# Attention, then a mixture of experts: six groups of the expert loop unrolled ahead of it, their scatters and first weights spread over the steps

## The chip, the cores and the metric

The kernel runs on one core of one Trainium2 chip. The metric is device time in microseconds; the kernel before took 1812.24 us, the median of three runs (1812.14 to 1816.8).

## The reference

Four batches of 12,288 queries (width 128) attend over 768 pooled keys each, which are also the values. Every one of the 49,152 resulting rows x then goes through a mixture of experts: it is kept as it is where its skip score is not positive, and otherwise gets the output of one of eight experts (the largest of eight logits), weighted by its gate, added.

```python
kv_pool = kv.reshape(B, H // r, r, W // r, r, C).mean(axis=(2, 4))
k = v = kv_pool.reshape(B, -1, C) @ w_sr
a = softmax(scale * (q @ k.T)); x = (a @ v).reshape(B * N, C)
do_compute = x @ w_skip > 0
e_idx = argmax(xc @ w_gate); gate_w = softmax(xc @ w_gate)[e_idx]      # xc = x[do_compute]
out = x;  out[do_compute] = xc + gate_w * (relu(xc @ w1[e_idx]) @ w2[e_idx])   # w1: 128x1024, w2: 1024x128
```

With the inputs used, each batch goes as a whole to one expert (batches 0, 2 and 3) or is skipped (batch 1).

## The kernel before, in words

**Phase 1, attention.** It is unrolled into 384 steps of 128 queries. A step multiplies the scores (`scores`, lines 625 to 627, PE), takes the row maximum (`row_max`, line 633, DVE), exponentiates (`row_exp`, line 639, ACT), and splits the probabilities into two 16-bit parts (`p_hi`, line 643, ACT; `p_lo`, line 647, DVE), which SP transposes by DMA into `pt` (line 652). Six steps later `attend` (line 690, PE) multiplies with the values; `scale` (line 705, ACT) normalizes the rows. Twelve steps make a round, 32 in all. For each round `route` computes each row's expert, gate and place: PE counts the rows per expert with one-hot matrices (line 808), DVE writes the places to `di` (line 843), and POOL writes the 12 row tiles, one indirect DMA each (`scatter_rows`, line 187), to a DRAM buffer `scr` that is sorted by expert. Through round 27 `route` is cut into slots, a piece a step, and up to round 29 the scatters go one a step; the last rounds run without slots, the very last in three parts whose small work is on DVE. The order on each engine is the program's (`manual_schedule`), so what is written first is issued first.

**Between the phases.** After round 26 `snapshot` looks for the expert with most rows so far. Twenty steps before attention's end `first_step` loads its number and its first row into SP's registers (lines 883 and 884) and asks for its weights; sixteen steps before the end it takes the maxima of the weights (`w_scale`, line 198), eleven before it splits w1 into two 16-bit parts (`split_w1`, ACT and POOL), eight before it prepares the first x (`x_transpose`, lines 253 to 264). `peel` then computes one group of 2048 rows of this expert, in four blocks of 512, while the last rounds are still being routed: an up half (`up`, 24 matmuls of 512 columns, lines 271 to 273, with ACT's `h_hi` and DVE's `h_lo` behind each three), and a down half. In the first three blocks `down` keeps w2 in place (line 287), ACT copies the result to `yT` (line 290), PE transposes it back (line 320), and `finish` adds (line 323) and scatters to the output by POOL. The fourth block has the loop's form, `down_rows` (line 300, 96 matmuls of 128 columns into four row tiles). `make_table` (lines 332 to 354) makes the list of all groups from the final counts; when it is done `flush` asks for the first weights and rows of the loop, and each engine loads the trip count `cumi` (line 1055).

**Phase 2, the loop.** A `For_i` loop takes one group per iteration, 17 here after the peeled one, in four blocks each. A block begins with `finish_rows` of the block before (line 311 on DVE, four output scatters on POOL), runs up and down, and in between loads the block's successor's rows (line 193, SP), prepares an xT two blocks ahead (`x_transpose`) and, over the iteration, the next expert's weights.

Of the kernel before, what the change touches and what calls it, by code (L numbers as in the profile page):

```python
# [20 lines left out]
RT = 12  # L21
# [3 lines left out]
def kernel(  # L25
# [29 lines left out]
    K1, K2 = 3, 2  # L55
    XP = 3
    XP2 = 4
# [62 lines left out]
    oh_few = [consts.tile([P, GT + 1, E], BF16, name=f"oh_few{i}") for i in range(2)]  # L120
    for x in oh_few:
        nc.gpsimd.memset(x, 0.0)

# [9 lines left out]
    snap = consts.tile([1, 2], F32, name="snap")  # L133
    snap_i = consts.tile([1, 2], I32, name="snap_i")
# [21 lines left out]
    w_max = wp.tile([P, 2], F32, name="w_max")  # L156
    w_dg = wp.tile([P, 2, P], BF16, name="w_dg")
# [3 lines left out]
    yT = wp.tile([P, ST], F32, name="yT")  # L161
# [3 lines left out]
    h = {}  # L165
# [9 lines left out]
    writes, first_writes, finished, ready, loaded, moved = [], [], [], [], [], []  # L175
# [19 lines left out]
    def w_scale():  # L195
        em = emask.broadcast_to([P, 2])
        for i, w in enumerate((w1_raw, w2_raw.rearrange("p k c -> p (k c)"))):
            nc.vector.tensor_reduce(out=w_max[:, i:i + 1], in_=w, axis=AX.X, op=ALU.max, apply_absolute_value=True)
# [17 lines left out]
    def split_w1(pool=False):  # L216
        nc.scalar.activation(out=w1_hi, in_=w1_raw, func=AF.Copy, scale=w_sc[:, 0:1])
        if pool:
            nc.gpsimd.tensor_scalar(out=w1_raw, in0=w1_raw, scalar1=w_sc[:, 0:1], scalar2=None, op0=ALU.mult)
            nc.gpsimd.tensor_tensor(out=w1_lo, in0=w1_raw, in1=w1_hi, op=ALU.subtract)  # L220
            return
# [29 lines left out]
    def x_transpose(s, pool=False):  # L251
# [3 lines left out]
        if pool:  # L255
            x = op.tile([P, TT, C], F32, name="o")
            nc.gpsimd.tensor_tensor(out=x, in0=xin[s][:, :, 0:C], in1=xin[s][:, :, C + 2:C + 3].broadcast_to([P, TT, C]),
                                    op=ALU.mult)
            nc.gpsimd.tensor_tensor(out=x16[:, 1, :, :], in0=x, in1=x16[:, 0, :, :], op=ALU.subtract)
        for t in () if pool else range(TT):  # L260
# [5 lines left out]
    def up(s, cs):  # L266
        hi, lo = (xT[s][:, i * TT:(i + 1) * TT, :].rearrange("p t x -> p (t x)") for i in range(2))
        for c in cs:
# [6 lines left out]
            nc.vector.scalar_tensor_tensor(out=h["lo"][:, c, :], in0=ps, scalar=0.0, in1=h["hi"][:, c, :],  # L275
                                           op0=ALU.max, op1=ALU.subtract)

    def down(s):
        ps = alloc["y"]()
        terms = []  # L280
        for c in range(FC + DL):
            if c < FC:
                terms += [(w2_hi, "hi", c), (w2_lo, "hi", c)]
# [123 lines left out]
    with ExitStack() as p1:  # L407
# [310 lines left out]
        def route(r, a, b, last, eng):  # L718
# [25 lines left out]
            if slots:  # L744
                yield 0
# [380 lines left out]
```

## Time and profile before

| | |
|---|---|
| three runs | 1812.14, 1812.24, 1816.8 us; median 1812.24 |
| profiled execution | 1808.65 us, its span 1805.3 us |
| busy share of the span | PE 95%, DVE 88%, ACT 71%, POOL 54% |
| granted PE clock, mean | 0.986 |
| scatters by POOL | 384 to `scr`, 288 to the output |

The profile is one execution. Its span is what the rows below are measured in; the execution's time is 3.35 us more, and the median of the runs 3.6 us more than that execution. Shares of busy time are means over stages of unlike kinds, so the rows are to be read by their place in time: attention until about 974 us, the transition until about 1070 us, the loop after that.

### The profile page before, as it was taken

The numbers are of one execution on the slowest core, as the hardware profiler recorded it, in microseconds if no ns is written. First come the engines' busy times: TensorE is split into PE (matmuls) and PEld (weight loads), VectorE is DVE, ScalarE is ACT, GpSimd is POOL, SyncE is SP. The second block draws the span as 40 slices with busy tenths as digits, with TensorE's granted clock in tenths as the row PEclk, the third lists the DMA queues.
The fourth block names the chain that finished last, engine by engine and source line by source line (L and its number), as shares of the span: only waits on it lengthen the run. The fifth ranks groups of instructions, "written<-read, shape, count | busy, mean of one in ns | idle before, by whom it ended". The sixth has DMA issues, their size and how long they took to land. (4 is left out here: it accounts for less than half of the span.)

```text
span 1805.3 us, 51758 instructions
## 1 busy us (share of the span) xinstructions
PE 1722.0 (95%) x18628; PEld 1424.7 (79%) x18628; DVE 1581.0 (88%) x3325; ACT 1272.9 (71%) x2415; POOL 982.2 (54%) x1246
## 2 busy tenths in 40 slices
PE   4999999999999999999998479999999999999998
PEld 3999999999999999999987147777777777777776
DVE  7999999999999999999997278888888888888887
ACT  2888888888888888888876245665566556665664
POOL 2168956878667787566556623433344334433443
PEclk9999999999999999999999789999999999999999
DMA  7999999999999999999997133433333333334333
GB/s 188 206 214 234 203 202 235 233 211 176 175 205 208 235 212 197 210 233 228 222 209 151 55 105 91 107 97 96 103 95 97 97 104 95 97 96 104 97 106 84
DMA packets 621974, 284.91 MB, mean 158 GB/s; under 512 B 503168, under 2 KB 571904, under 8 KB 621824
## 3 DMA queue, kind: packets, MB, share of 16 engines
q1 hardware_dynamic: 600320, 244.56, 67.0%
q0 software_dynamic: 21504, 38.43, 7.1%
q8 instruction: 84, 1.38, 0.3%
q14 instruction: 66, 0.54, 0.1%
HBM read 90.60 MB, written 78.64 MB: 94 GB/s over the span
## 5 line engine op out<-in xcount | busy, mean ns | idle before, releaser
L187 POOL DMA_INDIRECT out_dram<-o,xin x288 | 292.9, 1017 | 482.5 <-DVE o L311 384.7
L274 ACT ACTIVATE h_hi<-h_ps 128x512 f16<-128x512 f32 x544 | 317.2, 597 | 298.6 <-PE h_ps L273 277.4
L187 POOL DMA_INDIRECT scr<-rows,di x384 | 417.1, 1086 | 202.4 <-DVE nm L633 127.0
L639 ACT ACTIVATE p_sb<-s_ps,nm 128x768 f32<-128x768 f32 x384 | 346.5, 902 | 119.2 <-DVE nm L633 105.2
L633 DVE TENSOR_REDUCE nm<-s_ps 128x1 f32<-128x768 f32 x384 | 365.1, 951 | 21.2 <-PE s_ps L627 13.0
L275 DVE SCALAR_TENSOR_TENSOR h_lo<-h_ps,h_hi 128x512 f16<-128x512 f32 x544 | 348.5, 687 | 27.7 <-ACT h_hi L274 27.2
L690 PEld LDWEIGHTS <-pt 128*128 128x128 f16 x4608 | 275.7, 97 | 66.0 <-issue 62.7
L690 PE MATMUL acc_ps<-v_hi,pt 128*128 128x138 f16 x3072 | 320.9, 224 | 3.1 <-DMA pt<-p 1.9
L625 PE MATMUL s_ps<-k_hi,q_hi 128*128 128x384 f32 x768 | 293.6, 382 | 0.0
L690 PE MATMUL acc_ps<-v_lo,pt 128*128 128x138 f16 x1536 | 293.3, 223 | 0.0
L647 DVE SCALAR_TENSOR_TENSOR p<-p_sb,p 128x512 f16<-128x512 f32 x384 | 286.1, 745 | 5.4 <-ACT p L643 4.9
L300 PEld LDWEIGHTS <-h_hi 128*128 128x128 f16 x4416 | 275.8, 98 | 16.3 <-issue 1.5
L626 PE MATMUL s_ps<-k_lo,q_hi 128*128 128x384 f32 x768 | 260.5, 339 | 0.0
L627 PE MATMUL s_ps<-k_hi,q_lo 128*128 128x384 f32 x768 | 259.9, 338 | 0.0
L643 ACT ACTIVATE p<-p_sb 128x512 f16<-128x512 f32 x384 | 242.2, 631 | 14.1 <-DMA pt<-p 11.4
L300 PE MATMUL acc_ps<-w_hi,h_lo 128*128 128x128 f16 x2208 | 213.4, 219 | 0.0
L271 PE MATMUL h_ps<-xT,w_hi 128*128 128x512 f16 x544 | 207.3, 381 | 5.4 <-issue 4.9
L272 PE MATMUL h_ps<-xT,w_hi 128*128 128x512 f16 x544 | 207.4, 381 | 0.0
L273 PE MATMUL h_ps<-xT,w_lo 128*128 128x512 f16 x544 | 207.2, 381 | 0.0
L300 PE MATMUL acc_ps<-w_lo,h_hi 128*128 128x128 f16 x2208 | 202.9, 219 | 0.5 <-issue 0.3
L300 PE MATMUL acc_ps<-w_hi,h_hi 128*128 128x128 f16 x2208 | 202.0, 219 | 0.0
L690 PE MATMUL acc_ps<-v_hi,ptq 128*128 128x138 f16 x1536 | 178.2, 223 | 0.5 <-issue 0.5
(207 smaller groups left out, 2920.2 us busy)
## 6 DMA issues: line engine op xcount, KB each, us to landing
kvt<-in_kv_dram SPq DMA_DIRECT2D x96, 256.0 KB
q_sb<-in_q_dram SPq DMA_DIRECT2D x96, 256.0 KB
out_dram<-rows SPq DMA_DIRECT2D x96, 256.0 KB
xin<-scr SPq DMA_DIRECT2D x75, 264.0 KB, 2.9
w_raw<-in_moe_w_dram SPq DMA_DIRECT2D x38, 512.0 KB, 4.5
scr<-pad SPq DMA_DIRECT2D x32, 264.0 KB
pt<-p SPq DMA_TRANSPOSE x384
scr<-rows,di POOLq DMA_INDIRECT x384
```

Source lines behind the costliest of these rows:

```text
L187: ins = nc.gpsimd.indirect_dma_start(out=dst, out_offset=bass.IndirectOffsetOnAxis(ap=ids, axis=0), in_=src, in_offset=None, bounds_check= ...
L274: nc.scalar.activation(out=h["hi"][:, c, :], in_=ps, func=AF.Relu)
L275: nc.vector.scalar_tensor_tensor(out=h["lo"][:, c, :], in0=ps, scalar=0.0, in1=h["hi"][:, c, :], op0=ALU.max, op1=ALU.subtract)
L300: nc.tensor.matmul(ys[t], h[x][:, k, t * P:(t + 1) * P], w[:, k, :], start=(i == 0), stop=(i == len(terms) - 1))
L625: nc.tensor.matmul(s[:, h, :HK], q_hi, k_hi[:, sl], start=True, stop=False)
L626: nc.tensor.matmul(s[:, h, :HK], q_hi, k_lo[:, sl], start=False, stop=False)
L627: nc.tensor.matmul(s[:, h, :HK], q_lo, k_hi[:, sl], start=False, stop=True)
L633: paced["by"] = nc.vector.tensor_reduce(out=NM[t], in_=S_PS[t][:, :, :HK], axis=AX.XY, op=ALU.max, negate=True).ins
L639: nc.scalar.activation(out=P_SB[t], in_=S_PS.pop(t)[:, :, :HK], func=AF.Exp, bias=NM.pop(t))
L643: nc.scalar.activation(out=P16[t][:, 0, :], in_=p_flat(t)[:, 0:KD * P], func=AF.Copy, scale=2.0 ** PEXP)
L647: paced["both"] = nc.vector.scalar_tensor_tensor(out=p16[:, 1, :], in0=p_flat(t)[:, 0:KD * P], scalar=2.0 ** PEXP, in1=p16[:, 0, :], op0=A ...
L690: nc.tensor.matmul(ps[:, j % 2, :], w, v[a][:, k, :], start=(i == 0), stop=(i == len(AVL) - 1))
```

## The change

`peel` becomes six groups, 24 blocks, all in the loop's form: `down_rows` takes the name `down` and `finish_rows` the name `finish`, and the old forms with `yT` are gone. A peeled block's result stays in a pool of its own (`first_p`, six buffers) together with a copy of the row numbers (`kept`), so that the tile `xin` is free at once; the output scatters go to a list `out_rows`. All rounds are routed in slots, on POOL, and their scatters go to a list `scr_rows`. `scatter_next` takes one scatter from the lists: one a step in attention, five a block in the peel (at its top, in up at c = 0, 1 and 3, in down at d = 1), the oldest `scr` scatter first unless more than twenty output scatters wait. What is left in the list after the last block is issued before the trip count is loaded. The table is made in pieces among the first blocks. In the peel the next block's x is prepared at c = 3; `w_scale` for the loop stands in the up half of block 21 and block 22 (blocks are counted from 0), `split_w1` ahead of the last block's down.

The snapshot gives the first rows of up to six groups, in four pieces, and SP loads seven values in place of two. The first weights are prepared in small parts: maxima in halves, 16 to 11 steps before attention's end; w1 in quarters on ACT and POOL, 10 to 7 before it; the first x in quarters, 6 to 3 before it. The loop's code is unchanged but for the names.

```diff
-    def w_scale():
+    def w_scale(halves=False):
...
+            if halves:
+                for j in range(2):
+                    nc.vector.tensor_reduce(out=w_part[:, i, j:j + 1], in_=w[:, j * FF // 2:(j + 1) * FF // 2], axis=AX.X,
+                                            op=ALU.max, apply_absolute_value=True)
+                    yield
...
+    def finish(s):
+        o = (first_p[0] if first_p else op).tile([P, TT, C], F32, name="o")
...
+        if first_p:
+            kept = first_p[0].tile([P, TT], I32, name="ids")
+            nc.vector.tensor_copy(kept, ids[:, :, C + 1])
+            out_rows.extend((out, kept[:, t:t + 1], o[:, t, :], NT - 1, "out") for t in range(TT))
+            return
...
+    def scatter_next():
+        if scr_rows and len(out_rows) <= (HOLD - 1) * TT:
+            *row, whole = scr_rows.pop(0)
+        elif out_rows:
+            row, whole = out_rows.pop(0), False
+        else:
+            return
+        tc.add_manual_dep(scatter_rows(*row), paced["by"].name, sync_dep, reason="spread over the steps")
...
     def peel():
-        for s in range(NST):
+        LB = PEEL * NST
+        for b in range(LB):
+            s, last = b % NST, b == LB - 1
+            if b > 0:
+                for _ in finish((b - 1) % NST):
+                    pass
+                if b + 3 < LB:
+                    load_rows(snaps[1 + (b + 3) // NST], (b + 3) % NST, first_writes, "scr_first")
+                else:
+                    finished.append((b + 3) % NST)
+                yield "top", 0
             for c in range(FC):
                 up(s, [c])
...
+                if c == XP:
+                    if b == 0:
+                        split_w2()
+                    gates(s)
                     x_transpose((s + 1) % NST)
...
+                if b == LB - 3 and c == 5:
+                    scale = w_scale()
+                if b in (LB - 3, LB - 2) and c == 5:
                     next(scale, None)
-                yield
-            if s == NST - 1:
+                yield "up", c
+            if last:
                 split_w1()
-            if s == NST - 1:
+                x_transpose(1)
+            if b == 0:
                 ys.extend(acc_ps()[:, 0:C] for _ in range(TT))
...
+            for d, _ in enumerate(down(s)):
+                yield "down", d
...
-            di = small_t("di", I32)
+            di = dp.tile([P, RT], I32, name="di")
...
+            scr_rows.extend((scr, di[:, j:j + 1], rows[:, j, 0:ROW], E * CAP - 1, "scr", r == SNAPR and j == RT - 1)
+                            for j in range(RT))
...
             if left == 20:
...
                 e = nc.sync.value_load(snap_i[0:1, 0:1], min_val=0, max_val=E - 1)
-                st = nc.sync.value_load(snap_i[0:1, 1:2], min_val=0, max_val=E * CAP - G)
-                snaps.extend((e, st))
+                snaps.append(e)
+                for i in range(1, 1 + PEEL):
+                    snaps.append(nc.sync.value_load(snap_i[0:1, i:i + 1], min_val=0, max_val=E * CAP - G))
...
-            if left in (16, 13):
-                scales.append(scales.pop() if scales else w_scale())
+            if left in (16, 15, 14, 13, 12, 11):
+                scales.append(scales.pop() if scales else w_scale(True))
                 next(scales[0], None)
-            if left == L1:
-                split_w1(PW)
-            if left == L2:
-                x_transpose(0, PX)
+            if left in (10, 9, 8, 7):
+                sl = slice((10 - left) * FF // 4, (11 - left) * FF // 4)
+                nc.scalar.activation(out=w1_hi[:, sl], in_=w1_raw[:, sl], func=AF.Copy, scale=w_sc[:, 0:1])
+                behind(nc.gpsimd.tensor_scalar(out=w1_raw[:, sl], in0=w1_raw[:, sl], scalar1=w_sc[:, 0:1], scalar2=None,
+                                               op0=ALU.mult))
...
+        for kind, c in first:
+            if kind == "down" and c < 3:
+                run_jobs(None)
+            if kind == "top" or (kind == "up" and c in (0, 1, 3)) or (kind == "down" and c == 1):
+                scatter_next()
+            if not ready and not jobs and not scr_rows:
+                ready.append(True)
             flush()
+        assert loaded
+        while out_rows:
+            scatter_next()
```

On SP, twenty steps before attention's end, between a transpose of `p` and the loads of the first weights (`w_raw`), there stood before:

```order
L595 DMA q_sb<-in_q_dram 128x512
L883 TENSOR_LOAD snap_i
L883 ISA x2
L884 TENSOR_LOAD snap_i
L884 ISA x2
L237 ISA
L237 DMA w_raw<-in_moe_w_dram 128x1024
```

and now, with the first loads and the last row ahead of the next transpose:

```order
L583 DMA q_sb<-in_q_dram 128x512
L820 TENSOR_LOAD snap_i
L820 ISA x2
L823 TENSOR_LOAD snap_i
L823 ISA x2
...
L237 DMA w_raw<-in_moe_w_dram 128x1024
L240 ISA
L240 DMA w_raw<-in_moe_w_dram 128x8x128
L640 DMA_TRANSPOSE pt<-p_18434 128x8x128
```

The pair of line 823 stands there six times, so seven loads go ahead of the weights and the next transpose.

On DVE, in the peel, `h_lo` stood before in pairs between the pieces of the last round's routing (line 843 writes `di`):

```order
L275 SCALAR_TENSOR_TENSOR h_lo<-up_ps,h_hi 128x512 x2
L843 TENSOR_REDUCE di<-acc 128x4
L783 TENSOR_REDUCE mn<-ev 128x4
L785 TENSOR_TENSOR oh<-em_82,mn 128x32
L739 TENSOR_TENSOR oh_few_91<-oh,act 128x32
L275 SCALAR_TENSOR_TENSOR h_lo<-up_ps,h_hi 128x512 x2
```

From the fifth block on a block now reads as follows (line 293 finishes the block before, line 256 prepares the next block's x):

```order
L293 SCALAR_TENSOR_TENSOR o<-acc_ps,g_sc,xin_132 128x128 x4
L298 COPY ids<-xin_132 128x4
L270 SCALAR_TENSOR_TENSOR h_lo<-up_ps,h_hi 128x512 x4
L288 TENSOR_SCALAR g_sc<-xin_133,y_sc 128x4
L256 SCALAR_TENSOR_TENSOR x_136<-xin_134,x_136 128x128 x4
L270 SCALAR_TENSOR_TENSOR h_lo<-up_ps,h_hi 128x512 x4
```

The routing is gone from these blocks, and x stands behind the fourth `h_lo`.

On POOL, at the end of the peel, the scatters before stood thus (line 1055 loads the trip count):

```order
L187 DMA scr<-rows,di 409600x132 x4
L187 DMA out_dram<-o,xin_137 49152x128 x4
L187 DMA out_dram<-o,xin_138 49152x128 x4
L1055 TENSOR_LOAD cumi
```

and now:

```order
L183 DMA scr<-rows,di 409600x132 x10
L183 DMA out_dram<-o,ids 49152x128 x4
L183 DMA scr<-rows,di 409600x132
...
L183 DMA out_dram<-o,ids 49152x128 x76
L1006 TENSOR_LOAD cumi
```

Of the 76 output scatters, the last six are written behind the peel's last matmul and wait for it.

## Rows read from the trace of the kernel before

**Rows 1.** The page's busy tenths of PE in 40 equal slices of the span.

```profile
PE   4999999999999999999998479999999999999998
```

**Rows 2.** Windows of 10 us across the stretch between attention and the loop, all engines: window in us, its length, busy us (instructions) of PE, PE's weight loads, DVE, ACT and POOL, then the granted PE clock, DMA share, GB/s.

```profile
1000.00:1010.00 10.00, 0.00 (x0) 0.00 (x0) 0.00 (x0) 0.54 (x1) 7.58 (x11) 0.58 0.16 54
...
1020.00:1030.00 10.00, 3.37 (x14) 1.06 (x11) 0.34 (x1) 0.00 (x0) 7.59 (x11) 0.77 0.14 47
1030.00:1040.00 10.00, 3.24 (x9) 1.50 (x10) 2.93 (x11) 4.28 (x10) 1.76 (x2) 0.50 0.07 20
```

**Rows 3.** Timeline of PE, single rows: start us, us, engine, line, operation, tiles, shape, count, and in brackets the idle time before it with what ended it. The last score matmul; the last down matmul of block 0 and the first up matmul of block 1; the last matmul of the peeled group and the first of the loop; the first matmul of the loop's second block; the first matmuls of two blocks that follow each other later in the loop.

```profile
973.81 0.34 PE L627 MATMUL s_ps<-k_hi,q_lo 128*128 128x384 f32 x1
...
994.34 0.59 PE L287 MATMUL acc_ps<-h_lo,w_hi 128*128 128x512 f16 x2
...
994.77 0.38 PE L271 MATMUL up_ps<-xT,w_hi 128*128 128x512 f16 x1
...
1065.12 0.61 PE L300 MATMUL acc_ps<-w_lo,h_hi 128*128 128x128 f16 x8
...
1070.65 0.59 PE L271 MATMUL h_ps<-xT,w_hi 128*128 128x512 f16 x1 [4.92 <-issue]
...
1084.11 0.38 PE L271 MATMUL h_ps<-xT,w_hi 128*128 128x512 f16 x1
...
1201.15 0.38 PE L271 MATMUL h_ps<-xT,w_hi 128*128 128x512 f16 x1
...
1211.69 0.38 PE L271 MATMUL h_ps<-xT,w_hi 128*128 128x512 f16 x1
```

**Rows 4.** What line 1122 issued (the loop's branch hints on PE): duration in ns as min/median/max, first and last start in us.

```profile
L1122 PEldq BRANCH_PREFETCH_HINT  x17: 31/31/40, 1070.3 to 1753.9; - x17
```

**Rows 5.** Waits from 975 to 1065 us, all engines: who waited for what, us in total, times, the longest.

```profile
DVE di L843 <- DMA scr<-rows,di: 12.5, 1, 12.5
PE acc_ps L808 <- DVE oh L785: 12.3, 1, 12.3
```

**Rows 6.** Timelines of PE, POOL and ACT from 1018 to 1037 us, one row of each (columns as in Rows 3): the last matmul of block 1's down, one of the scatters that POOL issues meanwhile, and the activation that reads what that down made.

```profile
1019.66 0.59 PE L287 MATMUL acc_ps<-h_lo,w_hi 128*128 128x512 f16 x2
...
1024.42 0.98 POOL L187 DMA_INDIRECT out_dram<-o,xin  x1 [0.30 <-issue]
...
1035.66 0.69 ACT L290 ACTIVATE yT<-acc_ps,y_sc 128x512 f32<-128x512 f32 x1 [19.46 <-remote]
```

**Rows 7.** Groups of instructions on DVE in 1200 to 1242 us, four blocks of the loop: line, engine, operation, tiles, shapes, count, busy us in all and mean ns of one, idle time before them in us with what ended it.

```profile
L275 DVE SCALAR_TENSOR_TENSOR h_lo<-h_ps,h_hi 128x512 f16<-128x512 f32 x32 | 20.5, 687 | 1.6 <-ACT h_hi L274 1.6
L261 DVE SCALAR_TENSOR_TENSOR x<-xin,x 128x128 f16<-128x128 f32 x16 | 4.5, 343 | 0.0
L311 DVE SCALAR_TENSOR_TENSOR o<-acc_ps,g_sc,xin 128x128 f32<-128x128 f32 x16 | 4.5, 343 | 4.1 <-PE acc_ps L300 4.1
...
L198 DVE TENSOR_REDUCE w_max<-w_raw 128x1 f32<-128x1024 f32 x2 | 2.3, 1209 | 0.0
```

**Rows 8.** Timeline of DVE in one block of the loop, which begins at 1201.15 (columns as in Rows 3).

```profile
1201.04 1.12 DVE L311 SCALAR_TENSOR_TENSOR o<-acc_ps,g_sc,xin 128x128 f32<-128x128 f32 x4 [1.00 <-PE acc_ps L300]
1202.79 2.48 DVE L275 SCALAR_TENSOR_TENSOR h_lo<-h_ps,h_hi 128x512 f16<-128x512 f32 x4 [0.64 <-ACT h_hi L274]
...
1206.81 0.15 DVE L249 COPY y_sc<-y_sc 128x1 f32<-128x1 f32 x1
...
1209.52 1.13 DVE L261 SCALAR_TENSOR_TENSOR x<-xin,x 128x128 f16<-128x128 f32 x4
```

**Rows 9.** The transposes of xT in 1200 to 1242 us: from issue to landing.

```profile
DMA to landing us min/median/max: 3.3/3.4/3.5
```

**Rows 10.** Timeline of POOL at the loop's entry: two scatters one behind the other (columns as in Rows 3).

```profile
1074.85 0.97 POOL L187 DMA_INDIRECT out_dram<-o,xin  x1 [0.30 <-issue]
1076.12 0.97 POOL L187 DMA_INDIRECT out_dram<-o,xin  x1 [0.30 <-issue]
```

**Rows 11.** Line 1055, the load of the loop's trip count into an engine's register, on POOL and on SP (columns as in Rows 4).

```profile
L1055 POOLq TENSOR_LOAD <-cumi x1: 496/496/496, 1058.6 to 1058.6; - x1
...
L1055 SPq TENSOR_LOAD <-cumi x1: 820/820/820, 1067.7 to 1067.7; - x1
```

**Rows 12.** The row maxima of line 633, one per step of attention, in 919 to 976 us (the last 20) and in 809.5 to 870 us (26 of them) (columns as in Rows 4).

```profile
L633 DVE TENSOR_REDUCE nm<-s_ps x20: 894/950/958, 919.2 to 975.7; 128x1 f32<-128x768 f32 x20
...
L633 DVE TENSOR_REDUCE nm<-s_ps x26: 949/957/958, 809.8 to 869.5; 128x1 f32<-128x768 f32 x26
```

**Rows 13.** Timelines of SP, DVE, ACT and DVE again in attention's last 20 steps (columns as in Rows 3).

```profile
924.95 0.38 SPq L237 DMA_DIRECT2D w_raw<-in_moe_w_dram  x1
...
930.45 2.56 DVE L198 TENSOR_REDUCE w_max<-w_raw 128x1 f32<-128x1024 f32 x2
...
934.74 0.63 ACT L643 ACTIVATE p<-p_sb 128x512 f16<-128x512 f32 x1 [3.44 <-DMA pt<-p]
...
961.97 0.23 DVE L839 RECIPROCAL rows<-gs 128x12 f32<-128x12 f32 x1 [2.83 <-POOL gs L739]
```

**Rows 14.** Lines 883 and 884, the loads of the snapshot's expert and of its first row into SP's registers (columns as in Rows 4).

```profile
L883 SPq TENSOR_LOAD <-snap_i x1: 637/637/637, 923.2 to 923.2; - x1
...
L884 SPq TENSOR_LOAD <-snap_i x1: 282/282/282, 924.2 to 924.2; - x1
```

**Rows 15.** Waits of SP's queue from 1100 to 1790 us, all in the loop (columns as in Rows 5).

```profile
SPq L193 <- DMA out_dram<-o,xin: 150.2, 75, 3.5
```

More of the change, by code (lines that the diff above doesn't have):

```diff
@@ L254, in x_transpose @@
                                  scale=xin[s][:, t, C + 2:C + 3])
[L255 to L260, printed above, removed]
+        for t in range(TT):
             nc.vector.scalar_tensor_tensor(out=x16[:, 1, t, :], in0=xin[s][:, t, 0:C],
@@ L794, in route @@
-            gs = small_t("gs")
-            def gate_sum():
-                nc.vector.tensor_reduce(out=gs, in_=ex, axis=AX.X, op=ALU.add)
-            if not slots:
-                gate_sum()
-            ps = acc_ps()
-            w = n * E
-            nxt = ends if last else rt.tile([P, E], F32, name="nxt")
+            yield
+            pool("tensor_tensor", out=ohb, in0=oh, in1=bc(act), op=ALU.mult)
+            yield GT - 1
+            while accs.get("done", 0) != r:
+                yield GT - 1
@@ L836, in route @@
-            accs["done"] = r * RT + b
-            pool("tensor_tensor", out=acc, in0=acc, in1=ohb[:, 0:n, :], op=ALU.mult)
-            yield (0 if slots else None)
+            wa = E * RTP
+            ohf = oha.rearrange("p e t -> p (e t)")
+            nc.tensor.matmul(ps[:, 0:wa], ones_bf, ohf, start=True, stop=True)
+            nc.tensor.matmul(ps[:, wa:2 * wa], upper_bf, ohf, start=True, stop=True)
+            yield 0
+            gs = small_t("gs")
+            nc.vector.tensor_reduce(out=gs, in_=ex, axis=AX.X, op=ALU.add)
@@ L839, in route @@
+            pool("tensor_scalar", out=gs, in0=gs, scalar1=1e-9, scalar2=x_sc, op0=ALU.add, op1=ALU.mult)
+            accs["done"] = r + 1
+            if r == LASTR:
+                jobs.append([make_table(), None])
+            yield
+            pool("tensor_tensor", out=acc, in0=acc, in1=em(run), op=ALU.add)
+            pool("tensor_tensor", out=acc, in0=acc, in1=ohb, op=ALU.mult)
+            yield 0
             nc.vector.reciprocal(rows[:, :, C], gs)
-            if not slots:
-                yield
@@ L851, in route @@
-            for j in range(n):
-                if j > 0 and r < LASTR - 1:
-                    yield
-                ins = scatter_rows(scr, di[:, j:j + 1], rows[:, j, 0:ROW], E * CAP - 1, "scr")
-                if r < LASTR - 1:
-                    tc.add_manual_dep(ins, paced["by"].name, sync_dep, reason="one a step")
-            if r == SNAPR:
-                first_writes.extend(writes)
+            yield
+            nc.gpsimd.tensor_copy(rows[:, :, C + 2], x_sc.broadcast_to([P, RT]))
@@ L1035 @@
             taken.clear()
+            if live:
+                scatter_next()
             ranked = run_jobs(ph)
+            if not live and not taken:
+                scatter_next()
             if preps and not ranked and (ph != 0 or tb < LAG):
@@ L1091 @@
                         split_w1()
-                    for _ in down_rows(s):
+                    for _ in down(s):
                         pass
```

299 lines of the change are left out of this document (101 added, 198 removed).

## Prediction, before the change was run

> **What bounds the kernel now.** I read the page first, then the windows around the dip in it, then single rows there. In [rows 1] PE's slices stand at 9, except the first, the last and three (8, 4 and 7) past the middle: attention and the loop are PE-bound, and only the stretch between them is not. [rows 2] opens that stretch: PE is busy 0.00 us of 1000 to 1010, 3.37 and 3.24 of the two from 1020 to 1040, and the granted clock falls to 0.50. [rows 3] gives its ends. The last score matmul ends at 973.81 + 0.34 = 974.15; I call that S. Block 0's last down matmul begins at 994.34 and the first up matmul of block 1 at 994.77, so block 0 ends 20.6 us after S. The loop's first branch hint on PE is at 1070.3 [rows 4], 96.2 us after S. Between the two lies one group of four blocks, and the loop does a group in (1753.9 - 1070.3) / 16 = 42.73 us. The first iteration is slower: its first block takes 1084.11 - 1070.65 = 13.46 against 1211.69 - 1201.15 = 10.54 later [rows 3], 2.9 us more; the others so take 42.55, or 10.64 a block.
>
> What stands in the 96.2 us? [rows 5]: DVE waits 12.5 us for `di`, a short table that the last rounds' scatters still read, and PE's L808 waits 12.3 us behind that for a one-hot. [rows 6]: ACT starts yT at 1035.66, though PE's last matmul for it (1019.66 + 0.59) ended at 1020.25: 15.4 us in which no engine gives a reason, while POOL issues scatters. At the end PE stops at 1065.73 and restarts at 1070.65 [rows 3].
>
> **The change, part by part.** *Removed.* The 96.2 us, and five iterations of the loop: 5 x 42.55 = 212.8. That five go and not fewer rests on the first expert filling six groups at the snapshot, when 27 of 32 rounds (41,472 rows) are counted; the loop's 17 hints are one group less than all, so 18 groups run, and by the reference's routing each whole batch of 12,288 rows is six groups of one expert.
>
> *Added: 24 blocks in a row.* Block 0 takes its 20.6 us of [rows 3], with the attention's last six attends beside it. Its down now has `g_sc` and every round's routing in pieces beside it; no row prices that, so I add 1.4 and keep 0 as the lower end. Sum 22.0. The other 23 run the loop's form: 24 up and 96 down matmuls, the same columns. The lower price is the clean 10.54 of [rows 3], the mean of all iterations 10.64; I take 10.6: 243.8.
>
> Does DVE keep up? In a stretch of four loop blocks [rows 7] h_lo costs 20.5, x 4.5 and o 4.5 us of 42: 7.4 a block. The kept ids are one short copy, some 0.15 us like L249's in [rows 8]. PE sets the pace unless the next block's xT is late. The chain in a block that starts at T = 1201.15 [rows 8]: `o` ends at 1202.16, four h_lo take 2.48 from 1202.79 on, so with ids and g_sc before x the four x pieces (1.13) would be done at about T + 5.7; the transpose lands at most 3.5 later in this stretch [rows 9], T + 9.2. It is wanted at T + 10.54: 1.3 us to spare. In the order, x stands behind the first four h_lo, as I assumed.
>
> One block breaks this: `w_scale` sits in the middle of block 21. Its two w_max take 2.3 us of DVE [rows 7], ahead of three h_lo, and its small instructions come on top. Against 1.3 to spare I charge 2.0 and keep 0 as the lower end (the loop has the same work after up, beside 96 matmuls). split_w1 and x_transpose(1) stand before the last down and are hidden there (5.3 us).
>
> *Scatters.* Five per block at a pitch of 1.27 us (0.97 and 0.30 ahead of it, [rows 10]) are 6.4 us of POOL in 10.6, so POOL's queue keeps up; `di` has four buffers and nothing waits for it now. The queue is not empty at the end: six `out` scatters stand behind the last matmul, ahead of POOL's load of the trip count. Five pitches and one of 0.97 are 7.3; the load costs 0.5 [rows 11], and from the end of SP's load (1068.5) to the hint passed 1.8 before [rows 4, 11]: 9.6 for the loop's entry in all. PE stood still 4.9 there before, so its slow first block stays as it was.
>
> From S to the loop: 22.0 + 243.8 + 2.0 + 9.6 = 277.4, against 96.2 + 212.8 = 309.0. Gain 31.6.
>
> *Before S.* The last 19 steps take 975.7 - 919.2 = 56.5 us; 25 steps earlier take 59.7, so 19 should take 45.4 [rows 12]: 11.1 us of excess. I can name 3.4 (ACT waits for a transpose that was queued behind SP's value loads and weight loads) and 2.8 (DVE waits for `gs`, which POOL does behind the unquartered split) [rows 13]. After: the second wait goes. But SP's value loads go from two to seven. The second costs 924.95 - 924.2 = 0.7 to the next DMA [rows 13, 14], so five are +3.6, on the queue that carries every pt transpose. And w_max, 2.56 us that ran while ACT stood waiting [rows 13], is now in halves on a DVE that is full. 3.4 + 3.6 + 2.6 = 9.6: S comes 1.5 earlier. Lower end -8 (only the 3.4 stays), upper end +6 (the loads' wait comes on top of all else).
>
> Here a rule speaks against the change. The Trainium skill, page "DMA: Bandwidth & Descriptors", section "Latency and other measured facts", gives a `tensor_load` a floor of about 600 ns; the loads here took 637 and 282 ns [rows 14], so the second is under that floor, and by the page the five more would cost some 1.6 us more than I charge, an estimate.
>
> Sum: -31.6 - 1.5 = -33.1. The profiled execution took 1808.65 us (span 1805.3), the median of the runs is 1812.24, 3.6 above it. Execution 1775.5, span 1772.2, median **1779**.
>
> **Rivals.** *A: a stall like the one before yT comes back once.* For it: 24 blocks of straight code with scatters on POOL, and the 15.4 us that [rows 6] don't explain. Against: it happened while scatters went back to back, and now there are five to a block. Time 1779 + 15.4 = 1794. If the stall was the engine waiting for its code, it belongs to unrolled code, and there is six times as much now. The Trainium skill, page "Runtime: NRT & Kernel Launch", section "Instruction fetch mechanics", says that code in a straight line is fetched ahead and the boundary mostly hidden, and that a taken branch is what breaks this; by that page this rival would have no chance, and the trace does not decide it.
>
> *B: slower.* At the top of each block SP issues an xin load from scr. In the order, the loads of blocks 1 to 14 also wait for a scatter of POOL's queue. In the loop such a wait exists: SP's loads wait 150.2 us in 75 times for an `out` scatter, up to 3.5 [rows 15]. SP is in order and the xT transpose stands behind the load. Here the scatters are placed at fixed matmuls and `out` ones queue up behind `scr` ones; if POOL runs late, the load lands late, then the transpose, then PE. It decides once the wait passes the 1.3 us to spare: each us more costs 14. A wait of 3.7 us (2.4 x 14 = 33.6) eats the gain; one of 4.1 gives 1779 + 39 = 1818. Against it: POOL has 4.2 us free per block, and the load is issued 1 us into a block while the transpose wants to go at 5.7.
>
> *C: the peel is not full.* If the snapshot's expert had fewer than six groups, empty blocks would read pad rows and the loop would still run its 17 iterations: 1779 + 212.8 is about 1992. Against: the count of rows above.
>
> **How the numbers follow.** The forecast has 0.80, A 0.11, B 0.07 (0.04 of it slower, 0.03 about even), C 0.01; 0.01 is left for no change. Range: all low ends together (block 0 -1.4, blocks at 10.54 -1.4, w_scale -2, S -6.5) give 1767.7. Up, blocks at 11.0 (+9.2) and S at +6 (+7.5) give 1795.7, which takes in A. So 1767 to 1796. Repeated measurements tell 0.3% (5.4 us) from no change. Faster by more: 0.80 + 0.11 = 0.91; within: 0.04; slower: 0.05.
>
> **What would show it.** Right: 12 branch hints on PE, the first about 277 us after S; up matmuls of successive blocks 10.5 to 10.7 apart, PE at 9 in every slice from the middle on; no wait of several us for `di`; a gap of some 9 or 10 us on PE before the first hint, with six scatters in it. Wrong: a gap of 8 us or more inside the 24 blocks (A); blocks 1 to 14 longer than 15 to 23, with PE waiting for xT and SP for a scatter (B); 17 hints (C); row_max steps slower than 2.9 us in the last 20 (S).

## The result, and the profile after

The change is faster: ratio 0.9768, 95% interval 0.9751 to 0.9785. Three runs of it took 1770.28, 1770.41 and 1772.32 us (a fourth, in which the granted clock was 0.688 all through, is left out), against a median of 1812.45 before. The forecast was 1779, the range 1767 to 1796. Between the two profiled executions the step is smaller: 1808.65 to 1772.32, spans 1805.3 to 1770.4, that is 34.9 in the span against 33.1 forecast. The sum was made against the profiled execution, and that one lay 3.6 us below the median of its kernel's first three runs.

PE's slices on the page, against [rows 1]: the dip past the middle is gone; an 8 is left where attention ends (slice 22) and one at the loop's entry (slice 29).

```profile
PE   4999999999999999999998999999899999999998
```

The windows that answer to [rows 2] (same columns): PE is busy throughout, and the granted clock stays at 1.00.

```profile
1000.00:1010.00 10.00, 10.00 (x119) 7.41 (x118) 7.34 (x20) 5.28 (x14) 5.27 (x7) 1.00 0.39 90
...
1020.00:1030.00 10.00, 10.00 (x119) 7.50 (x118) 8.99 (x30) 4.95 (x12) 5.71 (x9) 1.00 0.38 86
1030.00:1040.00 10.00, 10.00 (x119) 7.42 (x118) 9.51 (x29) 4.96 (x13) 4.37 (x6) 1.00 0.42 67
```

The timeline of PE after the change, for [rows 3]: the last score matmul, the starts of blocks 1, 15, 16, 21, 22 and 23, the peel's last matmul and the loop's first, and the start of the loop's second block.

```profile
971.25 0.52 PE L615 MATMUL s_ps<-k_hi,q_lo 128*128 128x384 f32 x1
...
994.94 0.38 PE L266 MATMUL up_ps<-xT,w_hi 128*128 128x512 f16 x1
...
1143.18 0.38 PE L266 MATMUL up_ps<-xT,w_hi 128*128 128x512 f16 x1
...
1153.72 0.38 PE L266 MATMUL up_ps<-xT,w_hi 128*128 128x512 f16 x1
...
1207.92 0.38 PE L266 MATMUL up_ps<-xT,w_hi 128*128 128x512 f16 x1
...
1219.45 0.38 PE L266 MATMUL up_ps<-xT,w_hi 128*128 128x512 f16 x1
...
1231.40 0.38 PE L266 MATMUL up_ps<-xT,w_hi 128*128 128x512 f16 x1
...
1241.49 0.61 PE L281 MATMUL acc_ps<-w_lo,h_hi 128*128 128x128 f16 x8
1248.37 0.58 PE L266 MATMUL h_ps<-xT,w_hi 128*128 128x512 f16 x1 [6.28 <-issue]
...
1260.74 0.38 PE L266 MATMUL h_ps<-xT,w_hi 128*128 128x512 f16 x1
```

The loop's branch hints, for [rows 4]: twelve.

```profile
L1073 PEldq BRANCH_PREFETCH_HINT  x12: 31/31/40, 1247.9 to 1719.3; - x12
```

Where the 34.9 us came from, each term beside its forecast:

| term | forecast | measured |
|---|---|---|
| last score matmul (S) earlier by | 1.5 | 974.15 - 971.77 = 2.4 |
| block 0, from S | 22.0 | 994.94 - 971.77 = 23.2 |
| blocks 1 to 23, with w_scale | 245.8 | 1242.10 - 994.94 = 247.2 |
| last matmul to first hint | 9.6 | 1247.9 - 1242.1 = 5.8 |
| S to hint | 277.4 | 276.1 (before 96.2) |
| hint to the span's end | 212.8 less | 735.0 - 522.5 = 212.5 less |

### The profile page after: what moved, and what is told of

Its sections match the earlier page's. It is cut to its first block, busy times and chain, and to the rows that moved or that the text cites. A ratio compares the mean times of both kernels' runs of the same rounds, so it can differ in the third digit from the quotient of the medians.

```text
span 1770.4 us, 51397 instructions
## 1 busy us (share of the span) xinstructions
PE 1710.4 (97%) x18814; PEld 1431.1 (81%) x18814; DVE 1538.8 (87%) x3248; ACT 1255.0 (71%) x2403; POOL 971.9 (55%) x1262
## 5 line engine op out<-in xcount | busy, mean ns | idle before, releaser
L269 ACT ACTIVATE h_hi<-h_ps 128x512 f16<-128x512 f32 x384 | 223.9, 598 | 213.8 <-PE h_ps L268 186.0
L183 POOL DMA_INDIRECT out_dram<-o,xin x196 | 201.1, 1026 | 316.6 <-DVE o L293 264.4
L281 PEld LDWEIGHTS <-h_hi 128*128 128x128 f16 x4608 | 287.6, 98 | 18.7 <-issue 2.0
L635 DVE SCALAR_TENSOR_TENSOR p<-p_sb,p 128x512 f16<-128x512 f32 x384 | 276.2, 719 | 9.7 <-ACT p L631 7.2
L270 DVE SCALAR_TENSOR_TENSOR h_lo<-h_ps,h_hi 128x512 f16<-128x512 f32 x384 | 245.7, 687 | 23.8 <-ACT h_hi L269 18.1
L281 PE MATMUL acc_ps<-w_hi,h_lo 128*128 128x128 f16 x2304 | 222.9, 219 | 1.0 <-DVE h_lo L270 0.6
L281 PE MATMUL acc_ps<-w_hi,h_hi 128*128 128x128 f16 x2304 | 211.2, 219 | 2.6 <-ACT rows L693 1.8
L269 ACT ACTIVATE h_hi<-up_ps 128x512 f16<-128x512 f32 x192 | 106.5, 595 | 123.3 <-PE up_ps L268 118.9
L293 DVE SCALAR_TENSOR_TENSOR o<-acc_ps,g_sc,xin 128x128 f32<-128x128 f32 x288 | 81.0, 343 | 115.3 <-PE acc_ps L281 109.8
L678 PE MATMUL acc_ps<-v_lo,ptq 128*128 128x138 f16 x768 | 154.9, 223 | 0.0
```

The source lines that it names most:

```text
L183: ins = nc.gpsimd.indirect_dma_start(out=dst, out_offset=bass.IndirectOffsetOnAxis(ap=ids, axis=0), in_=src, in_offset=None, bounds_check= ...
L269: nc.scalar.activation(out=h["hi"][:, c, :], in_=ps, func=AF.Relu)
L270: paced["by"] = nc.vector.scalar_tensor_tensor(out=h["lo"][:, c, :], in0=ps, scalar=0.0, in1=h["hi"][:, c, :], op0=ALU.max, op1=ALU.subtra ...
L281: m = nc.tensor.matmul(ys[t], h[x][:, k, t * P:(t + 1) * P], w[:, k, :], start=(i == 0), stop=(i == len(terms) - 1))
L635: paced["both"] = nc.vector.scalar_tensor_tensor(out=p16[:, 1, :], in0=p_flat(t)[:, 0:KD * P], scalar=2.0 ** PEXP, in1=p16[:, 0, :], op0=A ...
L678: nc.tensor.matmul(ps[:, j % 2, :], w, v[a][:, k, :], start=(i == 0), stop=(i == len(AVL) - 1))
```

## The experiments

Two questions were open. Which part of the change pays: the six groups, or the scatters spread five to a block? And what were the 15.4 us of [rows 6]? **Theory 1**: a peeled block costs what a loop block costs, and what paid is that routing, table and `di` no longer stop the peel. **Rival 2**: unrolled groups pay by themselves. **Rival 3**: scatters back to back hold up the other engines, and spreading them is what paid.

**The kernel before, once more.** No edit.

> The kernel before, once more, for its trace. Theory 1: the 15.4 us in which ACT's yT stands still without a reason belongs to the program (the scatters back to back, the code of the peel), so it comes again at the same instruction within 1 us, and the span is 1805 within 3 us. Rival: it belongs to the one execution; then it is gone or stands elsewhere, the 96.2 us from the last score matmul to the loop's first hint are 80 to 85, and the spread of the runs of this kernel (1808.65 to 1816.8) is explained by where such a pause falls.

It took 1805.62 us, span 1802.3. The same two waits stood in the waits of 975 to 1065 us:

```profile
ACT yT L290 <- remote: 19.3, 1, 19.3
...
DVE di L843 <- DMA scr<-rows,di: 12.6, 1, 12.6
```

So the pause belongs to the program. In both traces POOL issues 29 scatters in one row around it (from 994.1 to 1032.1 us in the first). Yet the size of what the transition loses is not fixed. Beside four later groups of runs this kernel took 1807 (19 runs, 1800 to 1810), 1808, 1784 and 1787 (9 runs, 1784 to 1794). What the executions of 1784 to 1794 us skip stays open, since no trace shows one; their granted clock was 0.989 to 0.993 against 0.986 to 0.99 in the 19.

**Four groups, and scatters bunched.** Three kernels, timed together against the kernel before (median 1807.08).

```diff
-    PEEL = 6
+    PEEL = 4
```

> Four peeled groups in place of six, all else as in the change. Theory 1 (the gain is the transition that no longer stalls, and a peeled group costs what an iteration of the loop costs, 42.4 against 42.55): nothing is lost by the two groups themselves; 14 output scatters are left for the loop's entry in place of 6, eight more at 1.28 us, so the entry is up to 10 us longer, less what SP's own load already takes: 1776 to 1781, a ratio to before of 0.980 to 0.983. Rival 2 (unrolled groups are what pays, 34.9 us for five): two groups less lose 14 us on top of the entry, 1790 to 1795, 0.988 to 0.990.

Measured 1778.05, ratio 0.9856 (0.983 to 0.9881): the time is in Theory 1's window; the ratio is not, since the kernel before ran quicker beside it. The blocks keep 10.54 to 10.65 (w_scale's two aside), and what is lost stands at the entry, where 14 scatters are left:

```profile
1154.08 0.61 PE L281 MATMUL acc_ps<-w_lo,h_hi 128*128 128x128 f16 x8
1168.09 0.59 PE L266 MATMUL h_ps<-xT,w_hi 128*128 128x512 f16 x1 [13.40 <-issue]
```

This gap of PE is 13.4 in place of 6.28. Rival 2, which wanted 1790 to 1795, is out.

```diff
-            if kind == "top" or (kind == "up" and c in (0, 1, 3)) or (kind == "down" and c == 1):
+            if kind in ("top", "up", "down"):
```

> The change with a scatter placed at every step of a block (13 of them) in place of five, so that POOL issues scatters back to back from the last score on, about 35 to scr within the first three blocks, and none is left at the loop's entry. Theory 1 (what stalled before was that routing and the table were on the peel's path and that di had few buffers; the spreading itself is worth little): the first three blocks stay within 2 us in all, the entry gets 1 to 2 us shorter, 1769 to 1772, ratio 0.976 to 0.978. Rival 3 (scatters back to back hold up the other engines, as in the 15.4 us before): one or more pauses of over 8 us in blocks 0 to 2, 1779 or more, 0.982 or more.

Measured 1801.91 (10 runs), ratio 0.9975 (0.9963 to 0.9988): with all else of the change in place, bunching gives back most of the gain: the span is 1802.1 against 1770.4. Blocks 1, 2 and 4 take 21.5, 21.0 and 21.0 us. The windows of block 1, which begins at 997.28, while POOL issues eleven scatters in a row from 997.9 to 1011.7:

```profile
1000.00:1003.00 3.00, 3.00 (x23) 1.62 (x21) 3.00 (x9) 2.95 (x9) 2.17 (x3) 1.00 0.22 54
1003.00:1006.00 3.00, 1.73 (x29) 1.51 (x27) 2.47 (x6) 1.08 (x3) 2.31 (x3) 1.00 0.88 185
1006.00:1009.00 3.00, 0.65 (x3) 0.29 (x3) 0.00 (x0) 0.00 (x0) 2.39 (x3) 0.98 0.40 104
1009.00:1012.00 3.00, 1.24 (x7) 0.53 (x6) 0.00 (x0) 0.00 (x0) 2.31 (x4) 0.50 0.14 45
```

The columns are those of [rows 2]. In 1006 to 1009 PE runs three matmuls, DVE and ACT nothing, POOL its scatters; PE's gaps have no releaser but "issue", that is, the profile shows nothing that PE waited for. The granted clock falls to 0.50, the lower of its two levels (1.2 of 2.4 GHz), after PE does. Theory 1's second half falls, Rival 3 stands.

```diff
-    PEEL = 6
+    PEEL = 2
...
-            if kind == "top" or (kind == "up" and c in (0, 1, 3)) or (kind == "down" and c == 1):
+            if kind in ("top", "up", "down"):
```

> Two peeled groups in place of six, and a scatter at every step of a block, as in the run with 13 a block. Theory 1: two groups are enough to route the last rounds beside them; the same as that run within 3 us, 1768 to 1774, ratio 0.976 to 0.979. Rival 2 (unrolled groups pay by themselves, 7 us each): 28 us slower than it, about 1798, 0.992. A third way: the loop's first weights and rows are asked for only 3 blocks before the loop, and the entry waits for them: 2 to 8 us more.

Measured 1798.05 (10 runs), ratio 0.9955 (0.9937 to 0.9973), 3.9 quicker than the same with six groups; the last block before the loop lasts 15.2 with its entry against 15.6, so the third way did not come either. So four groups more bring nothing by themselves. What they bring are blocks over which 35 `scr` and 92 output scatters can be spread; that is argued from the counts, as two groups with five scatters a block were not run.

**How long a row, and where.** From here on most kernels have one run, and their totals also move where no edit stands. Over six traces whose code is the same up to S (the change among them) S lies anywhere from 969.5 to 976.2 us, and over the traces with twelve hints the stretch from hint to end takes 519.5 to 524.7. These runs are therefore read at their blocks. First eight scatters in a row at the block's top:

```diff
-            if kind == "top" or (kind == "up" and c in (0, 1, 3)) or (kind == "down" and c == 1):
+            for _ in range(8 * (kind == "top")):
```

> The change with eight scatters in one row at the top of each block until both lists are empty (blocks 1 to 7 get eight, later ones four), in place of five spread over the block. Theory 4 (PE's issue falls to a matmul every 0.5 to 1.2 us once POOL has issued scatters without a pause for about 7 us, and recovers some 2 us after the row ends): each row of eight lasts 10 us, so blocks 1 to 7 each lose 3 to 5 us, with PE gaps that begin 6.5 to 7.5 us after the row begins and that nothing releases; blocks 8 and on, with rows of four, stay at 10.5 to 10.7; 1790 to 1806 in all. Rival 5 (it takes a long row, as the 29 before, or rows while rounds are routed): blocks from 2 on stay within 1 us of 10.6, and the time is 1770 to 1775.

Measured 1818.59, span 1816.3. Blocks 1 to 7 take 16.8 to 17.5, 6.4 more than 10.54 and beyond the 3 to 5 expected; block 8, with a row of six, 13.0; later ones, with four, 10.54. Block 1 begins at 998.20; its row of eight and PE's gaps in it:

```profile
999.64 1.08 POOL L183 DMA_INDIRECT scr<-rows,di  x1 [3.92 <-DVE ids L298]
...
1008.66 0.97 POOL L183 DMA_INDIRECT scr<-rows,di  x1 [0.30 <-issue]
```

```profile
1005.39 0.33 PE L281 MATMUL acc_ps<-w_hi,h_hi 128*128 128x128 f16 x3
1006.84 0.22 PE L281 MATMUL acc_ps<-w_hi,h_hi 128*128 128x128 f16 x1 [1.12 <-issue]
1007.55 0.22 PE L281 MATMUL acc_ps<-w_hi,h_lo 128*128 128x128 f16 x1 [0.50 <-issue]
1008.26 0.34 PE L281 MATMUL acc_ps<-w_hi,h_lo 128*128 128x128 f16 x3 [0.49 <-issue]
1009.68 0.38 PE L281 MATMUL acc_ps<-w_lo,h_hi 128*128 128x128 f16 x4 [1.08 <-issue]
```

The gaps begin 6.1 us into the row, a little before Theory 4's 6.5 to 7.5. In 998 to 1131 us all of PE's waits stand in down, and none has a releaser:

```profile
PE acc_ps L281 <- issue: 30.3, 42, 1.4
```

They do not follow the 16 KB packets of the instruction queue that the trace holds: in block 1 one moves at 1003.5, before the gaps, and in block 7 (from 1100.25) none before 1112, though its gaps begin at about 1107.7.

A sixth scatter, in up:

```diff
-            if kind == "top" or (kind == "up" and c in (0, 1, 3)) or (kind == "down" and c == 1):
+            if (kind == "top" or (kind == "up" and c in (0, 1, 3)) or (kind == "down" and c == 1)) or (
+                    kind == "up" and c == 5 and not scr_rows):
```

> The change with a sixth scatter in each block (in up at c = 5) once all scr scatters are out, so that no output scatter is left for the loop's entry. By the prediction's term (six scatters, 7.3 us, ahead of the trip count's load) the gap on PE at the entry falls from 6.3 to about 2 or 3. By the trace after the change POOL's queue loads the count at 1244.84 with four scatters still to run, and SP has it at 1244.5, so only some 2 us hang on POOL: the gap falls to 4 to 4.9, as before the change, and the first block of the loop stays at 12 to 12.5.

Measured 1790.9, span 1789.2, some 19 us slower than the change, which neither side expected. The entry's gap fell to 4.78, as the trace had it. Of the difference 4.5 us lie ahead of S, which the edit does not touch. The rest is in the blocks: nine that now have a row of five take 11.7 to 11.9, and block 15, with a row of four that begins 4.6 us into it, 14.65. The block from 1094.73: the row's last two scatters and PE.

```profile
1100.02 0.98 POOL L183 DMA_INDIRECT out_dram<-o,ids  x1 [0.30 <-issue]
1101.49 0.98 POOL L183 DMA_INDIRECT out_dram<-o,ids  x1 [0.50 <-issue]
```

```profile
1101.92 0.22 PE L281 MATMUL acc_ps<-w_hi,h_hi 128*128 128x128 f16 x1
1103.30 0.33 PE L281 MATMUL acc_ps<-w_hi,h_hi 128*128 128x128 f16 x3 [1.16 <-issue]
```

Rows of eight in the down half:

```diff
-            if kind == "top" or (kind == "up" and c in (0, 1, 3)) or (kind == "down" and c == 1):
+            for _ in range(8 * (kind == "down" and c == 0)):
```

> The run with rows of eight scatters, but each row begins in the block's down half (behind its first 24 matmuls) in place of at the block's top; rows of eight in blocks 0 to 6 or so, rows of four after that. Theory 4 (age: PE falters when a row has run for 6 to 7 us, wherever it stands): the gaps begin 6 to 7 us after each row's start, that is in the next block's up half, and the rows of four in the later blocks cost nothing. Theory 7 (place: it is the down half, 96 short matmuls, that scatters disturb; the up half's long matmuls hide it): gaps within the down half itself, from 1 to 3 us after the row begins; the rows of four cost 1 to 3 us in each of some 15 blocks; 1795 or more.

Measured 1779.61, span 1777.6. Neither theory came. Blocks with a row of four that begins 6.9 us into the block (1089.82 in the block from 1082.86) stay at 10.54, so the down half as such is not it. Nor is it the row's age: rows of eight, sixteen, six, sixteen and twelve follow each other from block 0 on, the longest 20.5 us long, and PE has no pause without a releaser. Its waits in 999 to 1083 us are these, all of them:

```profile
PE up_ps L266 <- DMA xT<-x: 6.8, 3, 4.3
PE up_ps L762 <- POOL oh_all L724: 0.9, 1, 0.9
```

They, and a granted clock that falls to 0.50 after the longest of them, make blocks 1, 2, 5 and 6 longer (12.07, 12.93, 15.01 and 12.22). The waits for xT are Rival B's chain: the transpose stands on SP behind an `xin` load, which waits for a `scr` scatter in the long row.

```profile
SPq L189 <- DMA scr<-rows,di: 40.1, 5, 13.2
```

The sixth scatter behind down's last quarter, and w_scale behind up:

```diff
...
+            if b == LB - 3:
+                scale = w_scale()
+            if b in (LB - 3, LB - 2):
+                next(scale, None)
...
+                    kind == "down" and c == 3 and not scr_rows):
```

> The change with a sixth scatter in a block once the scr scatters are out, now behind the last quarter of down (it runs into the next block's row) in place of up's c = 5, where it cost 1.2 us a block; and w_scale for the loop moved behind up in blocks 21 and 22. Theory 7 (scatters hurt in the down half): the row of five now ends some 6 us into the block; the blocks with six fall from 11.75 to 10.5 to 10.9. Theory 4 (a row of five costs 1.2): they stay at 11.7. In both, blocks 21 and 22 fall from 11.5 and 11.95 to 10.5 to 11, and the entry's gap is 4.8.

Measured 1763.82, span 1761.8, the quickest of these. Of the 8.6 us of span that it is below the change, 3.9 lie between S and the hint, where the edits stand; the rest lies ahead of S and in the loop. Rows of five that begin 0.4 us into the block cost nothing (1098.89 to 1109.43 is 10.54):

```profile
1099.33 0.98 POOL L183 DMA_INDIRECT out_dram<-o,ids  x1 [1.70 <-PE acc_ps L281]
...
1104.55 0.98 POOL L183 DMA_INDIRECT out_dram<-o,ids  x1 [0.30 <-DVE x L256]
```

This row ends 6.6 us into its block. Blocks 21 and 22 fall to 10.65 and 11.47, the entry's gap to 4.74. For rows that begin in a block's first 2 us the runs line up by the row's end, counted from the block's start: ended at 6.3 or 6.6, loss 0; at 7.7, 1.2; at 8.8, 2.4; at 11.4, 6.4; at 14.4, 11. This is a count for such rows and no rule. Block 15 of this run has a row of five from 3.6 to 9.7 us into it and loses nothing; a row of four from 4.6 to 9.5 costs 4.1 in block 15 of the run with the sixth scatter in up, and nothing in block 16 of the run with the whole preparation (below). What in the chip slows PE, and why not in every long row, stays open. That the 15.4 us of [rows 6] are the same thing is likely and not shown: the kernel before was not run with its scatters spread.

**Attention's last steps.** Three kernels. `w1_lo` by one DVE instruction a quarter; five value loads moved to later steps; the preparation in one go, as before:

```diff
+                nc.vector.scalar_tensor_tensor(out=w1_lo[:, sl], in0=w1_raw[:, sl], scalar=w_sc[:, 0:1],
+                                               in1=w1_hi[:, sl], op0=ALU.mult, op1=ALU.subtract)
...
+            if left in (18, 16, 14, 12, 10):
+                i = (22 - left) // 2
+                snaps.append(nc.sync.value_load(snap_i[0:1, i:i + 1], min_val=0, max_val=E * CAP - G))
...
-            if left in (10, 9, 8, 7):
...
+            if left == 11:
```

> The change with the low part of w1 made by DVE, one instruction a quarter, in place of two on POOL. Theory 6 (in the last steps POOL, full with scatters, routing and the quarters, holds up DVE, which waits 0.97 and 3.30 us for gs and acc): these waits fall to under 1 us together, four instructions of some 0.35 us are added on DVE, and the last 20 row maxima come 2 to 3.5 us sooner than the 55.2 us (19 steps) of the change. Rival: DVE is full there, the four cost 1.4 and the wait stays with the routing: 0 to 1.5 us later.

Measured 1769.19. The last 19 steps took 53.4, and DVE no longer waited for POOL, so Theory 6 has the mechanism and nearly the size (1.8). But from S to block 1 it took 24.5 in place of 23.2, so most of it was given back.

> The change with the last five of SP's seven value loads moved to five later steps, one each (18, 16, 14, 12 and 10 steps before attention's end). By the prediction's term the five cost 3.6 us because they stand in one row ahead of a transpose of p; ACT waits 5.3 us in all for such transposes. Apart, each 0.7 us fits between two transposes: ACT's wait falls to 2 to 3.5 us as before the change, and the last 19 steps take 52 to 53.5 us in place of 55.2. Rival: the transposes are late because of the weights' transfers, not the loads; then the wait stays at 5 and the steps at 55.

Measured 1769.23. The wait for `pt` in 915 to 975 us, first in the change, then here:

```profile
ACT p L631 <- DMA pt<-p: 5.3, 2, 5.0
```

```profile
ACT p L631 <- DMA pt<-p: 3.2, 1, 3.2
```

The row maxima of the last 20 steps, first the change (55.2 for 19 steps), then here (52.6):

```profile
L621 DVE TENSOR_REDUCE nm<-s_ps x20: 944/949/958, 916.6 to 971.8; 128x1 f32<-128x768 f32 x20
```

```profile
L621 DVE TENSOR_REDUCE nm<-s_ps x20: 942/948/958, 919.2 to 971.8; 128x1 f32<-128x768 f32 x20
```

Five loads in one row cost some 2.6 us, less than the 3.6 of the sum; the six traces with the same code up to S have 54.2 to 55.7 for the 19 steps, so the step is larger than their spread. S itself stands only 0.2 sooner, as the steps before ended 2.6 later. (By the `tensor_load` floor of about 600 ns that the Trainium skill states in "DMA: Bandwidth & Descriptors", "Latency and other measured facts", the five would have cost 5.2, an estimate; the trace does not agree.)

> The change with the first weights and the first x prepared as before it: maxima in two goes, 16 and 13 steps before attention's end, w1 in one go on ACT and POOL 11 before, x in one go 8 before. By the prediction's terms this brings back the 2.8 us wait of DVE behind POOL and takes w_max (2.6) off the full steps: within 1 us of the 55.2 us for the last 19 steps. By the trace after the change, where DVE waits 0.97 and 3.30 us for POOL in spite of the quarters: the wait only moves, 54 to 57. Rival: the quarters pay, and the whole form costs 3 us or more, 58 to 60.

Measured 1770.96; the 19 steps took 57.5, between the two sides, so the quarters gain 2.3 there. But they bring the first xT later, and PE waits for it at the start of block 0. The first up matmul of block 0, in the change and then here:

```profile
976.93 0.39 PE L266 MATMUL up_ps<-xT,w_hi 128*128 128x512 f16 x1 [2.28 <-DMA xT<-x]
```

```profile
980.88 0.38 PE L266 MATMUL up_ps<-xT,w_hi 128*128 128x512 f16 x1
```

From S to block 1 this run takes 998.87 - 978.42 = 20.5 in place of 23.2. From the twentieth last row maximum to block 1 the two are alike, 77.9 here and 78.3 in the change: the quarters moved a wait and gained next to nothing.

**The edits that helped, together.**

```diff
+                x_transpose(1)
                 split_w1()
-                x_transpose(1)
```

with the sixth scatter at down's end, `w_scale` behind up in blocks 21 and 22, and the loads apart.

> The change with four edits at once, each read at its own place: the sixth scatter behind down's last quarter once the scr scatters are out, w_scale behind up in blocks 21 and 22, the last five value loads apart (these three as run before, one by one or in pairs), and in the last block x_transpose(1) ahead of split_w1. From the runs: blocks with six scatters stay at 10.5 to 10.9; blocks 21 and 22 at 10.6 and 11.5 (1.3 us less than in the change); ACT's wait for pt in the last steps 3 us and the last 19 steps 52 to 53.5 (2 us less); the gap at the entry, 4.7 with the sixth scatter, 3.2 to 4.2 with the transpose issued earlier. In all 5 to 7 us less than the change's 1770.3 to 1772.3: 1763 to 1766 (ratio to before depends on that kernel, which ran at 1784 to 1817). Rival: what is gained ahead of the loop is given back by chance pauses, as the last steps' gain with w1 on DVE was in block 0: 1768 to 1771.

Measured 1766.01 (5 runs, 1763.8 to 1766.97), ratio to the kernel before 0.9879 (0.9859 to 0.9899), the latter at a median of 1786.71 beside it. It is 4.4 us below the median of the change's own runs, which were taken at another time, so that step is not from one comparison. Between the profiled executions the stretch from S to the hint, where three of the four edits stand, is 4.0 us shorter. The 19 steps took 52.4, blocks with six scatters 10.54, blocks 21 and 22 10.54 and 11.46. The entry's gap stayed at 4.71: the earlier transpose brought nothing.

## Why the prediction was right

**The sum** held in its large terms. The five loop iterations were worth 212.5 against 212.8, and the 19 ordinary blocks of 1 to 22 (without 16, 21 and 22) average 10.59 against 10.6: the mechanism, blocks at the loop's price in place of a stretch that stands still, came as forecast. Its small terms erred by +1.2 (block 0), +1.4 (blocks 1 to 23) and -3.8 (the entry), and that they nearly cancel to 276.1 against 277.4 is luck.

**Block 0** took 23.2, outside its bounds of 20.6 and 22.0. The sum priced what joins it at 1.4 and had no wait for the first xT, which is now prepared 6 to 3 steps before attention's end in place of 8. That wait is 2.28; without it, in the run with the whole preparation, block 0 takes 20.5 with all that joins it.

**w_scale** cost 11.53 + 11.95 - 2 x 10.59 = 2.3 against 2.0; behind up it costs about 0.9.

**The entry** failed as a step. It said that all six scatters lie ahead of the trip count's load. POOL's sequencer loads it at 1244.8 while four scatters still wait in POOL, and SP had it at 1243.6:

```profile
1243.66 0.98 POOL L183 DMA_INDIRECT out_dram<-o,ids  x1 [0.30 <-issue]
...
1248.79 0.98 POOL L183 DMA_INDIRECT out_dram<-o,ids  x1 [0.30 <-issue]
```

```profile
L1006 SPq TENSOR_LOAD <-cumi x1: 887/887/887, 1243.6 to 1243.6; - x1
...
L1006 POOLq TENSOR_LOAD <-cumi x1: 657/657/657, 1244.8 to 1244.8; - x1
```

The last scatter begins after the hint at 1247.9. The six cost 1.5 (6.28 against 4.74 to 4.78 without them), not 7.3; eight more cost 7 in the run with four groups.

**Before S** the size was near (2.4 against 1.5) by luck. S moves by more than that over traces of the same code (969.5 to 976.2), and in the change the 2.4 lie ahead of the last 20 steps: their first row maximum stands 2.6 sooner (916.6 against 919.2), and from there to S it took 55.2 against 54.9. The working fails in three places. It names 6.2 of the 11.1 us of excess and lets the other 4.9 go without a reason. It charges five loads with 3.6 where they cost some 2.6. And it lets DVE's wait for POOL go; the wait is still there and longer, 3.3 and 1.0, since the quarters fill POOL in the steps in which it also routes:

```profile
DVE di L784 <- POOL acc L724: 3.3, 1, 3.3
...
DVE rows L782 <- POOL gs L724: 1.0, 1, 1.0
```

Its own sign of being wrong, row maxima slower than 2.9 us a step, was just met: 55.2 / 19 = 2.906.

**Rival A** named the right suspect (scatters back to back) and did not come, as five to a block leave gaps. Its chance hung on the placing alone, which the prediction did not price: bunched, the same code loses 31. Straight code was not the cause: PE's blocks ran at 10.54 in six groups of it. The Trainium skill, "Runtime: NRT & Kernel Launch", "Instruction fetch mechanics", says that crossing into the next piece of straight code is mostly hidden, and the trace agrees. Block 16 is longer, 11.77, without a reason that the profile shows: PE has two gaps without a releaser there, 0.8 us in all, while POOL's row slid to 4.6 to 8.2 us into the block. The same block with a row from 4.6 to 9.5 took 10.54 in another run, so this cause stays open. **Rival B** did not come: no block from 1 to 14 exceeds 10.85, though SP's loads do wait for a `scr` scatter, 40.3 us in ten times and up to 5.1. Its chain is real, as the rows of eight in down showed. **Rival C** did not come: 12 hints.

**What lay outside the sum** is the spread of the kernel before: the median fell by 42.0 where the profiled executions fell by 36.3. Its time rests on how much the pauses take in a run, and beside the last experiment its median was 26 below the first. So the 0.9768 holds for the runs that it was taken from; beside a kernel before at 1787 the change's 1770 would be about 0.99, an estimate from runs taken at different times.

## What to carry to other kernels

Indirect scatters that no engine waits for are not free: look at what PE does while they run back to back, place them a few at a time, and read the trace of each placing, since no rule for the place came out of these runs. When an unrolled stretch replaces loop iterations at the same price per block, look for the gain in the stalls that it can spread, and size it against runs whose own stalls you have seen more than once. An instruction behind others on a queue is not late by all of them, if the sequencer runs ahead of its engine, as POOL's did by four scatters here. And when a preparation is cut into small parts, follow its result to the first one who needs it: what the last steps gained in quarters, block 0 lost.

## What was not expected of the hardware

PE, with nothing to wait for that the profile shows, issues one to four short matmuls every 0.7 to 1.45 us while POOL issues a row of more than four or five scatters that began near the block's top, and DVE and ACT run dry behind it. A row of five shifted by 1 us costs 0 or 1.2 us a block. Rows of up to sixteen that begin in the down half did nothing of the kind. Which resource they share no run here shows.
